# One change to a fused scan and two-layer feed-forward kernel: weight conversion handed out by need, an earlier fetch of constants, and whole units for the second tile

## The chip, the cores and the metric

The kernel runs on one core of a Trainium2 chip. The metric is the device time of one execution in microseconds (us), lower is better; for the kernel before it is the median of three runs.

## What is computed

```python
log_a = np.log(np.clip(a, 1e-06, 1.0))
for c in range(nc):                      # chunks of 32 along the sequence of 768
    ...
    L = np.exp(cum[:, :, :, None] - cum[:, :, None, :]) * causal
    y_intra = np.einsum('bhij,bhjd->bhid', CB * L, xc)
    y_inter = np.einsum('bhin,bhnd->bhid', Cc, state) * decay_to_i
    state = decay_full * state + np.sum(Bx, axis=2)
x = y.transpose(0, 2, 1, 3).reshape(B * S, H * D)          # 3072 tokens x 256
h = np.maximum(np.maximum(x @ w1, x @ w2), x @ w3)         # 256 -> 768
x = h @ w_out                                              # 768 -> 256
h = x @ v_in                                               # 256 -> 2048
g = np.maximum(h, 0.0) + alpha * np.minimum(h, 0.0)
out = g @ v_out                                            # 2048 -> 256
```

The scan has 4 batches, 8 heads, head width 32 and state 16. The weights arrive in 64-bit floats.

## The kernel before

The tokens are cut into six tiles of 512. A tile goes through layer 1 (`up1`, L586: three products with 256-wide weights, their maximum) and layer 2 (`up2`, L600: one product and the leaky maximum), each followed by a product back to 256 columns (`down`, L613). A *unit* is one 128-wide slice f of a layer's hidden width over one tile: 6 in layer 1, 16 in layer 2. Every product is done in two halves of each operand (`parts`, L567, whose matmul is L572): high by high, low weight by high, high weight by low, so 18 matmuls for `up1` (three weights, two row halves), 6 for `up2`, 6 for `down` (two halves of the output columns). After `up` the unit's result g is split into gh on ScalarE (ACT, L123) and gl on GpSimd (POOL, L124), and `down` of a unit follows two units later (`LAG`).

The phases run in the order of `PHASES` (L32): layer 1 of tiles 0 and 1, then layer 2 of tile t and layer 1 of tile t + 2 in turn. Tiles 0 and 1 of layer 1 are cut into units of 256 tokens (`SPLIT`, in the order `ORDER`), all others into 512 (`WHOLE`).

Two other kinds of work are put between the units.

**Weight conversion** (`convert`, L158). The weights come in 28 pieces of 512 KB: 12 of layer 1, 16 of layer 2. One piece takes four steps: a shift on VectorE (DVE, L163), a merge of the two words (DVE, L165), then the fetch of the piece three ahead into the staging tile just freed (L149, on the queue of SyncE, SP) and the high half on ACT (L169), then the low half on DVE (L171) and, for the next piece, a rebias on ACT (L156). Three staging tiles `st` go round. Sixteen steps are taken ahead of the first unit; from there `pace` = 1 asks for one step at each of four places of a layer 1 unit (after each of its three products and after `down`) and two of a layer 2 unit.

**Attention** (the scan), in 24 blocks of 128 tokens, four to a tile. The list `todo` holds its steps; a block has six: loads (b and c, 64 KB each, x 128 KB, and the decay rows e, 256 KB), transposes `att_t` (matmul L331), the exponentials `att_e` (ACT L400, then a causal select on POOL, L403), the state update `att_u` (matmul L455, DVE L461 and L467), the products `att_b` (matmul L422, multiplied into e on DVE, L427), and the output `att_y` (matmuls L496 and L504, whose halves go to xt on ACT L513 and DVE L514). `quota` (L558) says how many steps follow a unit, so that each unit's blocks are done `LEAD` = 6144 matmul columns ahead of it; a unit of layer 1 needs all blocks up to its last token. From block 12 on a wider form is used, for which `wide_sums` (L277) makes prefix sums with two triangular constants of 128 KB; it fetches them itself (L280) just ahead of the matmuls that read them (L285).

Only the start (`with tc.manual_schedule()`, L665 to L718) keeps the order in which it is written. Behind it a scheduling layer orders each engine's instructions, so that a step may stand well ahead of the place at which the code asks for it. Engines run their own list in order.

Of the kernel before, what the change touches and what calls it, by code (L numbers as in the profile page):

```python
# [19 lines left out]
P = 128  # L20
# [7 lines left out]
NF1, NF2 = FF1 // P, FF2 // P  # L28
NT = BT * S // 512

SPLIT, WHOLE = ((0, 256), (256, 256)), ((0, 512),)
PHASES = [(1, 0, SPLIT, 1), (1, 1, SPLIT, 1)]  # L32
for _t in range(NT):
    PHASES += [(2, _t, WHOLE, 1)] + [(1, _t + 2, WHOLE, 1)] * (_t + 2 < NT)

LEAD = 6144
START = 4
LAG = 2
NX = 3

C_ID, C_PAR, C_PM, C_N = 0, 128, 130, 132
C_TU, C_TS, C_TW, C_SEL, C_T = 0, 128, 256, 512, 1024
# [29 lines left out]
def fused(ctx: ExitStack, tc: tile.TileContext, x, a, B, C, w1, w2, w3, w_out, v_in, v_out, alpha, cst, out):  # L72
    nc = tc.nc
# [103 lines left out]
    steps = convert()  # L177
    ready = [0]

    def need(i):  # L180
        while ready[0] <= i:
            next(steps)

    def next_weights(n):
        for _ in range(n):
            next(steps, None)


    cum_d = dr.tile([NQ, BT * H, Q], F32, name="cum_d", bufs=1)
# [57 lines left out]
    def sums(half):  # L247

        ks = slice(3 * half, 3 * half + 3)
        qs = slice(6 * half, 6 * half + 6)  # L250
        cols = slice(3 * P * half, 3 * P * (half + 1))
        pc = ptile(ps_at, "at", (BT * H, 3 * P))
        for k in range(3):
            nc.tensor.matmul(pc[:, k * P:(k + 1) * P], s_la[:, 3 * half + k, :], tri_u, start=True, stop=True)
        yield
        nc.vector.tensor_copy(s_tot[:, qs].unsqueeze(2), pc.rearrange("p (k i) -> p k i", i=Q)[:, :, Q - 1:Q])
        nc.vector.tensor_copy(s_cum[:, cols], pc)
        nc.sync.dma_start(cum_d[qs].rearrange("k h i -> h k i"), s_cum[:, cols].rearrange("h (k i) -> h k i", i=Q))
        yield
        pf = ptile(ps_at, "at", (P, BT, 6))  # L260
        for b in range(BT):
            nc.tensor.matmul(pf[:, b, :], s_c[:BT * H, C_SEL + b * P:C_SEL + (b + 1) * P], s_tot[:, qs], start=True, stop=True)
        nc.scalar.activation(dec_f[:, :, qs], pf, AF.Exp)
        yield
        pt = ptile(ps_at, "at", (P, 3, BT * H))
        for k in range(3):
            nc.tensor.transpose(pt[:, k, :], s_cum[:, (3 * half + k) * P:(3 * half + k + 1) * P], ident[:BT * H, :BT * H])
        nc.scalar.activation(dec_c[:, ks].rearrange("p k b h -> p k (b h)"), pt, AF.Exp)
        nc.scalar.activation(ncum[:, ks].rearrange("p k b h -> p k (b h)"), pt, AF.Copy, scale=-1.0)
        yield  # L270
# [5 lines left out]

    def wide_sums(half):  # L277

        if half == 0:
            nc.sync.dma_start(s_c[:, C_TW:C_SEL], cst[:, C_N + C_TW:C_N + C_SEL])  # L280
        ks = slice(3 * half, 3 * half + 3)
        cols = slice(3 * P * half, 3 * P * (half + 1))
        pc = ptile(ps_at, "at", (BT * H, 3 * P))
        for k in range(3):
            nc.tensor.matmul(pc[:, k * P:(k + 1) * P], s_la[:, 3 * half + k, :], s_c[:, C_TW:C_TW + P], start=True, stop=True)  # L285
        nc.scalar.activation(s_a[:, cols], pc, AF.Copy)
        nc.sync.dma_start(cum_w[:, cols], s_a[:, cols])
# [229 lines left out]
    def rounds(r0):  # L517

        for r in range(r0, NR):
            def first(r=r):  # L520
                if r + 1 < NR:
                    att_l(r + 1)
                if r + 2 < NR:
                    att_a(r + 2)
            yield first, 0
            yield lambda r=r: att_y(r), r + 1
            if r + 1 < NR:
                yield lambda r=r: att_e(r + 1), 0
# [20 lines left out]
    def units_of(ph):  # L549

        layer, t, tokens = ph[:3]
        if len(tokens) == 1:
            cut = [(f, 0, 512) for f in range(NF1 if layer == 1 else NF2)]
        else:
            cut = [(f, *tokens[h]) for q, h in ORDER for f in (2 * q, 2 * q + 1)]
        return [(f, o, n, (24 if layer == 1 else 12) * n, (4 * t + (o + n) // P) * (layer == 1)) for f, o, n in cut]

    def quota(i):  # L558

        most, ahead, own = 0.0, 0, plan[i][3]  # L560
        for _, _, _, cols, blocks in plan[i:]:
            most = max(most, left(blocks) * own / max(own, ahead - LEAD))
            ahead += cols
        return most


    def parts(acc, wh, wl, rhs, first, last):  # L567
# [16 lines left out]
        return gh[:, :n], gl[:, :n]  # L584

    def up1(ph, f, o, n):  # L586
        t, pace = ph[1], ph[3]
        fs = slice(f * P, (f + 1) * P)
        g = un.tile([P, 512], F32, tag="g", name="g")[:, :n]
        for j in range(3):  # L590
            need(4 * (f // 2) + j)
            p = up_mm([w[:, j, :, fs] for w in w123], xt[t], o, n)
            if j == 0:
                nc.scalar.activation(g, p, AF.Copy)  # L594
            else:
                nc.vector.tensor_tensor(g, p, g, ALU.max)  # L596
            next_weights(pace)
        return halves(g, n)

    def up2(ph, f, o, n):  # L600
        t, pace = ph[1], ph[3]
        fs = slice(f * P, (f + 1) * P)
        g = un.tile([P, 512], F32, tag="g", name="g")[:, :n]
        need(4 * (NF1 // 2) + 2 * (f // 2))
        p = up_mm([w[:, :, fs] for w in vi], yt[t], o, n)
        nc.vector.tensor_scalar(g, p, 0.0, alph[:, f:f + 1], ALU.min, ALU.mult)  # L606
        nc.vector.scalar_tensor_tensor(g, p, 0.0, g, ALU.max, ALU.add)  # L607
        next_weights(pace)
        return halves(g, n, nc.vector if t == NT - 1 and f == NF2 - 1 else nc.gpsimd)

    acc = {}
# [108 lines left out]
    if True:  # L720
        nc.sync.dma_start(alph, alpha.rearrange("(k p) -> p k", p=P))
        todo += [(go, 0) for go in (
            lambda: att_a(2), lambda: (att_t(2), load(3)), lambda: att_e(2),
            lambda: att_u(2), lambda: att_b(2), lambda: att_a(3), lambda: (att_t(3), load(4)),
        )]
        todo.insert(SUMS, (lambda: list(sums(1)), 0))
        todo += rounds(2)
        for i, go in enumerate((lambda: wide_sums(0), lambda: wide_sums(1), wide_back)):
            todo.insert(WIDE + 3 * i, (go, 0))
        plan = [u for ph in PHASES for u in units_of(ph)]  # L730

        owed, at = 0.0, 0
        for ph in PHASES:
            layer, t, _, pace = ph
            up, end = (up1, end1) if layer == 1 else (up2, end2)
            pend = []
            for f, o, n, _, blocks in units_of(ph):
                until(blocks)
                pend.append((f, o, n, up(ph, f, o, n)))
                if carry:  # L740
                    carry.pop(0)()
                elif tail:
                    tail.pop(0)()
                if len(pend) > LAG:
                    down(ph, *pend.pop(0))
                next_weights(pace)
                owed += quota(at)
                at += 1
                while owed > 0.999 and todo:
                    owed -= 1  # L750
                    attend()
            for i, u in enumerate(pend):
                def go(ph=ph, u=u, finish=end if i == LAG - 1 else None):
                    down(ph, *u)
                    if finish:
                        finish(ph)
                carry.append(go)
        for go in tail:
            go()
        tail.clear()  # L760
        for u in pend[:-1]:
            down(ph, *u)
        f, _, _, g = pend[-1]
        for o, n in SPLIT:
            down(ph, f, o, n, [x[:, o:o + n] for x in g])
            end2(ph, o, n)
            while tail:
                tail.pop(0)()
# [25 lines left out]
```

## Time and profile before

| | |
|---|---|
| median of 3 runs | 569.25 us (569.04 to 570.7) |
| the profiled execution | 569.79 us, of which the profile's span is 568.0 us |
| PE (TensorE matmul) busy | 553.3 us, 97% of the span |
| DVE / ACT / POOL busy | 338.4 / 234.7 / 226.9 us |
| granted TensorE clock | full in all 40 slices of the span |
| chain that ended last | PE 85%, DMA 8%, DVE 3% |

In a profile's row for a group of instructions, `x18` is a count, `[0.83 <-DVE e L427]` says that the engine stood idle for 0.83 us and what ended that, and a name such as `up<-xt,w` gives the tile written and the tiles read. A busy PE is not always PE at its best: a matmul's row lasts until its last result is out, while the next one has begun.

### The profile page before, as it was taken

The page shows a single profiled execution, that of the slowest core. Times are in us where ns is not written, and L with a number is a line of the kernel's source. Part 1 is how long each engine was busy: PE and PEld are TensorE (multiplying, and loading weights), DVE is VectorE, ACT ScalarE, POOL GpSimd, SP SyncE. Part 2 cuts the span into 40 slices and gives each one's busy share as a digit, 9 for nine tenths or more (in the row PEclk, how much of TensorE's full clock was granted, in tenths as well). Part 3 has the DMA queues.
Part 4 walks back from the last instruction along what each step waited for, and adds up shares of the span by engine and source line. Part 5 has one row for each costly group of instructions (what it writes and reads, how often), then busy time and mean ns, then how long its engine had stood idle before and what let it go on. Part 6 is the DMA issues. An engine that isn't in the chain of part 4 may idle for free.

```text
span 568.0 us, 10190 instructions
## 1 busy us (share of the span) xinstructions
PE 553.3 (97%) x3754; PEld 446.3 (79%) x3754; DVE 338.4 (60%) x633; ACT 234.7 (41%) x598; POOL 226.9 (40%) x238
## 2 busy tenths in 40 slices
PE   8989999999999999999999999999999999999996
PEld 4769798897777887777787887787777888888885
DVE  5887899847564446765546664545664325555553
ACT  5667679744233334242543333534322222223222
POOL 2144343445444235453324553423444123444441
PEclk9999999999999999999999999999999999999999
DMA  7888887612213426325354325244110010000001
GB/s 145 222 164 161 233 214 211 144 30 38 31 43 87 111 66 140 86 59 136 73 134 111 89 50 139 65 113 112 38 55 1 1 37 2 0 2 18 20 0 37
DMA packets 118928, 48.53 MB, mean 85 GB/s; under 512 B 80736, under 2 KB 108832, under 8 KB 118880
## 3 DMA queue, kind: packets, MB, share of 16 engines
q1 hardware_dynamic: 118880, 47.90, 34.8%
q8 instruction: 29, 0.48, 0.4%
q14 instruction: 19, 0.16, 0.1%
HBM read 39.82 MB, written 8.06 MB: 84 GB/s over the span
## 4 chain that ended last, share of the span: by engine, by line
PE 85%; DMA 8%; DVE 3%; ACT 2%; issue 1%; POOL 1%; SPq 0%; DVEq 0%; ACTq 0%; POOLq 0%
PE up L572 45%; PE acc L572 30%; DMA st<-in_moe_w_out_dram 4%; DMA b<-in_B_dram 2%; DMA st<-in_moe_w_in_dram 1%; PE at L412 1%; PE at L483 1%; PE up L648 1%; PE at L331 1%; PE at L504 1%; PE at L422 1%; DVE v L165 1%; DMA e<-cum_w 1%; PE at L496 1%; PE at L480 1%
## 5 line engine op out<-in xcount | busy, mean ns | idle before, releaser
L124 POOL TENSOR_TENSOR gl<-g,gh 128x512 fp32r<-128x512 f32 (+1 forms) x143 | 173.0, 1210 | 262.8 <-ACT gh L123 236.2
L123 ACT ACTIVATE gh<-g 128x512 fp32r<-128x512 f32 (+1 forms) x144 | 85.6, 594 | 239.1 <-DVE g L607 157.9
L572 PE MATMUL up<-xt,w 128*128 128x256 f32 (+1 forms) x864 | 166.0, 342 | 3.3 <-ACT g L594 2.7
L572 PEld LDWEIGHTS up<-xt,w 128*128 128x128 f32 x864 | 134.5, 189 | 25.4 <-ACT g L594 3.5
L572 PE MATMUL up<-yt,vi 128*128 128x512 f32 x576 | 151.1, 396 | 0.0
L572 PEld LDWEIGHTS up<-yt,vi 128*128 128x128 f32 x576 | 105.4, 188 | 24.0 <-issue 2.0
L606 DVE TENSOR_SCALAR g<-up,alph 128x512 f32<-128x512 f32 x96 | 72.0, 750 | 87.4 <-PE up L572 81.5
L572 PE MATMUL acc<-gh,vo 128*128 128x512 f32 (+1 forms) x388 | 119.6, 389 | 0.6 <-DVE yt L634 0.5
L596 DVE TENSOR_TENSOR g<-up,g 128x256 f32<-128x256 f32 (+1 forms) x96 | 53.2, 554 | 69.2 <-PE up L572 67.9
L572 PEld LDWEIGHTS acc<-gh,vo 128*128 128x128 f32 x388 | 72.2, 188 | 16.3 <-DVE yt L634 1.4
L572 PE MATMUL acc<-gl,vo 128*128 128x512 f32 (+1 forms) x194 | 75.2, 388 | 0.0
L607 DVE SCALAR_TENSOR_TENSOR g<-up,g 128x512 f32<-128x512 f32 x96 | 66.3, 691 | 3.0
L572 PE MATMUL acc<-gh,wo 128*128 128x256 f32 (+1 forms) x192 | 49.2, 342 | 0.4 <-ACT gh L123 0.2
L572 PEld LDWEIGHTS acc<-gl,vo 128*128 128x128 f32 x194 | 36.4, 188 | 7.8 <-DVE gl L124 0.2
L572 PEld LDWEIGHTS acc<-gh,wo 128*128 128x128 f32 x192 | 32.5, 190 | 4.4 <-ACT gh L123 0.4
L594 ACT ACTIVATE g<-up 128x256 f32<-128x256 f32 (+1 forms) x48 | 23.4, 487 | 30.3 <-PE up L572 27.3
L572 PE MATMUL acc<-gl,wo 128*128 128x256 f32 (+1 forms) x96 | 32.5, 338 | 0.0
L395 ACT ACTIVATE e<-e,ncum 128x128 f32<-128x128 f32 x96 | 30.4, 391 | 3.5 <-DMA e<-cum_w 3.5
L514 DVE TENSOR_TENSOR xt<-at,xt 128x128 fp32r<-128x128 f32 x48 | 11.9, 286 | 20.2 <-ACT xt L513 20.2
L165 DVE SCALAR_TENSOR_TENSOR v<-st,v 128x512 uint32<-128x512 uint32 x28 | 21.6, 773 | 1.0 <-ACT st L156 0.5
L396 POOL TENSOR_SCALAR_AFFINE_SELECT e<-e 128x512 f32<-128x512 f32 x24 | 15.7, 653 | 16.2 <-ACT e L395 12.9
L400 ACT ACTIVATE e<-e,ncum 128x64 f32<-128x64 f32 x80 | 21.4, 342 | 1.1 <-DMA e<-cum_d 1.0
(120 smaller groups left out, 440.3 us busy)
## 6 DMA issues: line engine op xcount, KB each, us to landing
e<-cum_w SPq DMA_DIRECT2D x24, 256.0 KB, 4.1
st<-sc SPq DMA_DIRECT2D x48, 128.0 KB, 2.6
st<-in_moe_w_out_dram SPq DMA_DIRECT2D x11, 512.0 KB, 4.5
st<-in_moe_w_dram SPq DMA_DIRECT2D x9, 512.0 KB, 5.0
sc<-ts SPq DMA_DIRECT2D x12, 384.0 KB, 2.3
st<-in_moe_w_in_dram SPq DMA_DIRECT2D x8, 512.0 KB, 4.4
v<-sc SPq DMA_DIRECT2D x48, 64.0 KB, 2.4
out_dram<-st SPq DMA_DIRECT2D x12, 256.0 KB, 2.2
```

Of the source, the lines that this page charges most:

```text
L123: nc.scalar.activation(dst_h, src, AF.Copy)
L124: engine.tensor_tensor(dst_l, src, dst_h, ALU.subtract)
L165: nc.vector.scalar_tensor_tensor(v, hi, 3, v, ALU.logical_shift_left, ALU.bitwise_or)
L395: nc.scalar.activation(e[:, q, :], e[:, q, :], AF.Exp, bias=ncum[:, k, b, 4 * g + q:4 * g + q + 1])
L396: nc.gpsimd.affine_select(out=e, in_=e, pattern=[[0, 4], [1, P]], compare_op=ALU.is_ge, fill=0.0, base=0, channel_multiplier=-1)
L400: nc.scalar.activation(e[:, h, :], e[:, h, :], AF.Exp, bias=ncum[:, k, b, h:h + 1])
L514: nc.vector.tensor_tensor(xt[t][1][:, g, o], yp[g], xt[t][0][:, g, o], ALU.subtract)
L572: nc.tensor.matmul(acc, w, r, start=(first and i == 0), stop=(last and i == len(todo_) - 1), skip_group_check=True)
L594: nc.scalar.activation(g, p, AF.Copy)
L596: nc.vector.tensor_tensor(g, p, g, ALU.max)
L606: nc.vector.tensor_scalar(g, p, 0.0, alph[:, f:f + 1], ALU.min, ALU.mult)
L607: nc.vector.scalar_tensor_tensor(g, p, 0.0, g, ALU.max, ALU.add)
```

## The change

1. Tile 1 of layer 1 is cut into 6 units of 512 tokens in place of 12 of 256.
2. Past tile 0 the conversion steps are handed out by `quota_w`: at each place (`slot`) a fraction of a step is added to `owing`, sized so that each unit's pieces are converted `LEADW` = 12288 columns ahead of it. A unit has four places: in layer 1 one after each product and one behind `down`, in layer 2 two and two. Worked out from the formula, a place takes 0.96 to 0.98 of a step in tile 1 of layer 1 and 0.47 to 0.50 in layer 2 of tile 0, up to its unit 11, where the last step falls. Tile 0 of layer 1 keeps one step at each place.
3. The fetch of the wide constants moves from `wide_sums` into the eighth attention step (the one with block 3's transposes and block 4's loads).

```diff
-PHASES = [(1, 0, SPLIT, 1), (1, 1, SPLIT, 1)]
+PHASES = [(1, 0, SPLIT, 1), (1, 1, WHOLE, 0)]
 for _t in range(NT):
-    PHASES += [(2, _t, WHOLE, 1)] + [(1, _t + 2, WHOLE, 1)] * (_t + 2 < NT)
+    PHASES += [(2, _t, WHOLE, 0)] + [(1, _t + 2, WHOLE, 0)] * (_t + 2 < NT)
...
+LEADW = 12288
...
+    owing = [0.0, 0.0]
+
+    def slot():
+
+        owing[0] += owing[1]
+        while owing[0] > 0.999:
+            owing[0] -= 1
+            next_weights(1)
...
-        if half == 0:
-            nc.sync.dma_start(s_c[:, C_TW:C_SEL], cst[:, C_N + C_TW:C_N + C_SEL])
...
+    def quota_w(i):
+
+        most, ahead, own = 0.0, 0, plan[i][3]
+        for _, _, _, cols, _, pieces in plan[i:]:
+            most = max(most, (4 * pieces - done[0]) * own / max(own, ahead - LEADW))
+            ahead += cols
+        return most / 4
...
-            next_weights(pace)
+            slot()
...
+        todo[7] = (lambda go=todo[7][0]: (go(), nc.sync.dma_start(s_c[:, C_TW:C_SEL], cst[:, C_N + C_TW:C_N + C_SEL])), 0)
...
             for f, o, n, _, blocks, _ in units_of(ph):
                 until(blocks)
+                owing[1] = pace or quota_w(at)
```

Since the first unit of tile 1 now holds all 512 tokens, it needs blocks 4 to 7 where it needed 4 and 5. By `quota`'s formula the attention steps behind a unit of tile 0, from its fourth unit on, rise from about 2.2 to between 3.0 and 3.5 (the last unit's fall to 0.9), and the output of blocks 6 and 7 and what lies between moves from tile 1 into tile 0.

What the scheduling layer makes of it stands in three places. On DVE, the end of the conversion: before, with L163, L165 and L171 the conversion, L596 the maximum of layer 1 and L606 and L607 those of layer 2 (names: v and st staging, vi and vo weights of layer 2, g a unit's result):

```order
L165 SCALAR_TENSOR_TENSOR v<-st,v 128x512
L596 TENSOR_TENSOR g<-up,g 128x256
L171 TENSOR_TENSOR vo_116<-v,vo_115 128x512
L596 TENSOR_TENSOR g<-up,g 128x256 x2
L514 TENSOR_TENSOR xt_1959<-at,xt_1958 128x128 x2
L596 TENSOR_TENSOR g<-up,g 128x256 x4
L461 TENSOR_TENSOR u<-at,ct 128x128
L467 SCALAR_TENSOR_TENSOR u<-u,dec_f 128x64 x2
L596 TENSOR_TENSOR g<-up,g 128x256 x2
L427 TENSOR_TENSOR e<-at,e 128x256 x2
L606 TENSOR_SCALAR g<-up,alph 128x512
L607 SCALAR_TENSOR_TENSOR g<-up,g 128x512
```

and now (L167 and L173 are the conversion, L617 the maximum of layer 1, L627 and L628 those of layer 2):

```order
L617 TENSOR_TENSOR g<-up,g 128x512
L167 SCALAR_TENSOR_TENSOR v<-st,v 128x512
L439 TENSOR_TENSOR e<-at,e 128x256 x2
L173 TENSOR_TENSOR vo_116<-v,vo_115 128x512
L617 TENSOR_TENSOR g<-up,g 128x512 x2
L362 TENSOR_TENSOR bs<-at,ct 128x256
L627 TENSOR_SCALAR g<-up,alph 128x512
L628 SCALAR_TENSOR_TENSOR g<-up,g 128x512
```

In both, the last piece is converted ahead of layer 2's first maximum, though the code now asks for 23 of the 112 steps behind that phase's start. Eight maxima of tile 1, those of four units of 256 tokens, stood behind the last conversion; now two, those of the last unit of 512. Ahead of tile 1's first maximum stand the low halves of 18 pieces in both.

On SP, the fetch of the wide constants (`yt<-in_shape_constants`; xm is x, e<-cum_d the decay rows, L149 and L151 fetch weights). Before, it is the 56th issue, behind the loads of block 6:

```order
L217 DMA xm_105<-in_x_dram 64x8x32 [waits DMAHW5_49,PE_49]
L217 DMA xm_105<-in_x_dram 64x8x32 [waits DMAHW6_49,PE_49]
L280 DMA yt_120<-in_shape_constants_dram 128x256 [waits DMAHW7_49]
L149 DMA st<-in_moe_w_in_dram 128x2x256 [waits DMAHW0_49,DVE_49]
L149 DMA st<-in_moe_w_out_dram 128x2x256 [waits DMAHW1_49,DVE_49,Activation_49]
L287 DMA cum_w<-xt_119 32x384 [waits DMAHW2_49,Activation_49]
```

and now the 41st, behind those of block 4:

```order
L231 DMA xm_106<-in_x_dram 64x8x32 [waits DMAHW6_49]
L231 DMA xm_106<-in_x_dram 64x8x32 [waits DMAHW7_49]
L749 DMA yt_120<-in_shape_constants_dram 128x256 [waits DMAHW0_49]
L151 DMA st<-in_moe_w_dram 128x2x256 [waits DMAHW1_49,DVE_49,Activation_49]
L325 DMA e<-cum_d 64x512 [waits DMAHW2_49]
```

It has moved ahead of three fetches of weights, two blocks' e and two blocks' b, c and x.

On PE, the seam of the tenth and eleventh of tile 0's twelve units (L593 was L572 before, L467 L455, L434 L422, L508 L496, L516 L504), where block 6's state and products stood before:

```order
L593 MATMUL acc<-gl,wo_111 128x256
L508 MATMUL at<-cpt,u 64x64 x4
L516 MATMUL at<-e,xm_105 32x64 x16
L467 MATMUL at<-xm_106,bp 32x128 x4
L593 MATMUL up<-xt_305,w_0_109 128x256
L434 MATMUL at<-cs,bs 64x128 x8
L593 MATMUL up<-xt_305,w_0_109 128x256
L593 MATMUL up<-xt_305,w_1_110 128x256 x2
L593 MATMUL up<-xt_306,w_0_109 128x256 x2
```

Here block 6's output and block 7's state and products follow one another; block 7's output stands one unit later. Before, both outputs stood in tile 1.

## Rows read from the trace of the kernel before

**Rows 1.** Windows: stretch, length, busy us (count) of PE, PEld, DVE, ACT, POOL; clock; DMA share; GB/s

```profile
35.87:78.64 42.77, 40.08 (x485) 34.95 (x483) 33.93 (x78) 31.03 (x97) 17.65 (x26) 1.00 0.83 195
78.64:113.50 34.86, 32.49 (x357) 29.46 (x356) 31.91 (x70) 27.90 (x80) 15.97 (x21) 1.00 0.73 188
113.50:125.09 11.59, 11.59 (x151) 10.66 (x150) 4.68 (x14) 6.11 (x22) 6.58 (x11) 1.00 0.16 35
...
175.65:212.55 36.90, 36.90 (x199) 29.74 (x198) 17.06 (x31) 13.94 (x33) 11.22 (x12) 1.00 0.33 84
```

**Rows 2.** Chain of waits, 113 to 126 us: start, us, what

```profile
114.21 0.40 PE at L496 x16
114.61 0.58 PE at L504 x32
115.20 2.34 PE up L572 x18
117.54 0.72 PE acc L572 x6
118.26 2.16 PE up L572 x18
...
121.14 0.36 PE at L455 x8
...
124.56 0.60 PE at L422 x16
```

**Rows 3.** Chain of waits, 175 to 190 us (layer 1 of tile 2)

```profile
175.82 4.08 PE up L572 x18
...
181.50 4.31 PE up L572 x18
...
185.82 1.36 PE acc L572 x6
...
187.65 0.33 PE at L331 x3
```

**Rows 4.** Timeline of PE, around 95 and 110 us: start, us, what [idle before]

```profile
95.47 1.77 PE L572 MATMUL up<-xt,w 128*128 128x256 f32 x12 [0.80 <-ACT g L594]
...
110.59 2.67 PE L572 MATMUL up<-xt,w 128*128 128x256 f32 x16 [1.37 <-ACT g L594]
```

**Rows 5.** Chain of waits, 85 to 130 us

```profile
102.13 5.95 DMA st<-in_moe_w_out_dram
```

**Rows 6.** Timeline of PE, 57 to 59 us

```profile
58.13 0.81 PE L285 MATMUL at<-yt,la 128*32 128x128 f32 x6 [0.88 <-DMA yt<-in_shape_constants_dram]
```

**Rows 7.** Timeline of SP, 44 to 62 us

```profile
54.90 0.61 SPq L280 DMA_DIRECT2D yt<-in_shape_constants_dram  x1
```

**Rows 8.** Line L165, 20 to 125 us: count, ns min/median/max, first and last start

```profile
L165 DVE SCALAR_TENSOR_TENSOR v<-st,v x25: 673/683/1236, 22.4 to 111.5; 128x512 uint32<-128x512 uint32 x25
```

**Rows 9.** Windows of L165 alone: stretch, length, busy us (count)

```profile
20.50:35.87 15.37, 3.72 (x5) 1.00 0.86 157
35.87:56.63 20.76, 3.43 (x4) 1.00 0.86 168
56.63:78.64 22.01, 4.28 (x6) 1.00 0.81 221
78.64:113.50 34.86, 8.12 (x11) 1.00 0.73 188
```

**Rows 10.** Timeline of POOL and DVE, 64 to 66 us

```profile
64.72 0.82 POOL L124 TENSOR_TENSOR gl<-g,gh 128x256 fp32r<-128x256 f32 x1 [4.91 <-DMA e<-cum_d]
64.86 1.22 DVE L171 TENSOR_TENSOR vo<-v,vo 128x512 fp32r<-128x512 f32 x1
```

**Rows 11.** Timeline of ACT, DVE and PE, 37 to 42 us

```profile
37.33 2.00 ACT L400 ACTIVATE e<-e,ncum 128x64 f32<-128x64 f32 x8
...
41.33 0.76 DVE L427 TENSOR_TENSOR e<-at,e 128x256 f32<-128x256 f32 x2 [0.75 <-POOL e L403]
...
41.91 0.45 PE L496 MATMUL at<-cpt,u 32*64 32x64 f32 x8 [0.83 <-DVE e L427]
```

More of the change, by code (lines that the diff above doesn't have):

```diff
@@ L178, in fused @@
     ready = [0]
+    done = [0]
     def need(i):
         while ready[0] <= i:
-            next(steps)
+            next_weights(1)
     def next_weights(n):
         for _ in range(n):
+            done[0] += 1
             next(steps, None)
+    owing = [0.0, 0.0]
[3 more added lines that the diff above has]
+            owing[0] -= 1
+            next_weights(1)
     cum_d = dr.tile([NQ, BT * H, Q], F32, name="cum_d", bufs=1)
@@ L555, in units_of @@
             cut = [(f, *tokens[h]) for q, h in ORDER for f in (2 * q, 2 * q + 1)]
-        return [(f, o, n, (24 if layer == 1 else 12) * n, (4 * t + (o + n) // P) * (layer == 1)) for f, o, n in cut]
+        return [(f, o, n, (24 if layer == 1 else 12) * n, (4 * t + (o + n) // P) * (layer == 1),
+                 4 * (f // 2) + 4 if layer == 1 else 4 * (NF1 // 2) + 2 * (f // 2) + 2) for f, o, n in cut]
     def quota(i):
         most, ahead, own = 0.0, 0, plan[i][3]
-        for _, _, _, cols, blocks in plan[i:]:
+        for _, _, _, cols, blocks, _ in plan[i:]:
             most = max(most, left(blocks) * own / max(own, ahead - LEAD))
@@ L586, in up1 @@
     def up1(ph, f, o, n):
-        t, pace = ph[1], ph[3]
+        t = ph[1]
         fs = slice(f * P, (f + 1) * P)
@@ L596, in up1 @@
                 nc.vector.tensor_tensor(g, p, g, ALU.max)
-            next_weights(pace)
+            slot()
         return halves(g, n)
     def up2(ph, f, o, n):
-        t, pace = ph[1], ph[3]
+        t = ph[1]
         fs = slice(f * P, (f + 1) * P)
@@ L607, in up2 @@
         nc.vector.scalar_tensor_tensor(g, p, 0.0, g, ALU.max, ALU.add)
-        next_weights(pace)
+        slot()
+        slot()
         return halves(g, n, nc.vector if t == NT - 1 and f == NF2 - 1 else nc.gpsimd)
@@ L736, in fused @@
             pend = []
-            for f, o, n, _, blocks in units_of(ph):
+            for f, o, n, _, blocks, _ in units_of(ph):
                 until(blocks)
+                owing[1] = pace or quota_w(at)
                 pend.append((f, o, n, up(ph, f, o, n)))
@@ L745, in fused @@
                     down(ph, *pend.pop(0))
-                next_weights(pace)
+                slot()
+                if layer == 2:
+                    slot()
                 owed += quota(at)
```

## The prediction

> **What bounds the kernel now.** I read the windows by stage first. They are cut where the first matmul of a phase starts: tile 0 of layer 1 at 20.5 us, tile 1 at 78.64, layer 2 at 125.09, tile 2 of layer 1 at 175.65. From 113.5 us on PE is busy all the time, in layer 1 of tile 2 for 36.90 of 36.90 us [rows 1]. Behind that point only fewer or shorter matmuls help, and the change keeps them. Ahead of it PE stands idle for 42.77 - 40.08 = 2.69 us in tile 0 (from its fourth unit) and for 34.86 - 32.49 = 2.37 us in tile 1 [rows 1], with DVE busy for 31.91 of those 34.86 us. So tiles 0 and 1 of layer 1 are the place, and little more than 5 us of idle PE lies there.
>
> The second view is the chain, for what a unit costs. One of 256 tokens takes 2.16 us for its 18 up matmuls, or 2.34 where attention has come between, and 0.72 for its 6 down [rows 2]. One of 512 takes 4.08 or 4.31, and 1.36 [rows 3]. The third is the timeline of PE at its longest waits: 0.80 and 1.37 us in tile 1, both ended by ACT's copy of a product [rows 4], with a weight piece's landing of 5.95 us in the chain ahead of the second [rows 5], and 0.88 us in tile 0 on the wide constants [rows 6]. The fourth is the merge of the conversion, L165: 25 of them from 22.4 to 111.5 us [rows 8], so 89.1 / 24 = 3.71 us a piece, but unevenly: 15.37 / 5 = 3.1, then 20.76 / 4 = 5.2, 22.01 / 6 = 3.7 and 34.86 / 11 = 3.2 [rows 9].
>
> **The change, part by part.** *Whole units in tile 1.* Like against like, 12 x (2.16 + 0.72) = 34.6 against 6 x (4.08 + 1.36) = 32.6 us, or 12 x (2.34 + 0.72) = 36.7 against 6 x (4.31 + 1.36) = 34.0. That is -2.0 or -2.7; I take **-2.4**, since both kinds occur. PE bounds tile 1's second half wholly [rows 1], so this lies on the path. A 256-column matmul costs 2.16 / 18 = 120 ns in the row and a 512-column one 227. The Trainium skill (TensorE: Matmul & The Clock Gate, section Back-to-back issue gap) gives 262 and 518 cycles for them, at 2.4 GHz 109 and 216 ns, so that width would be worth only 288 x 0.109 - 144 x 0.216 = 0.3 us, as an estimate of that page. The rows hold both widths, and they decide.
>
> *The wide constants.* The fetch was issued at 54.90 us [rows 7] and PE waited 0.88 us for it [rows 6]. It now stands 15 issues earlier on SP, two blocks' loads ahead, so it lands before it is asked for: **-0.9**, or 0 at the other end. What it is moved past (three fetches of weights, two blocks' loads) is put back once by one issue, 0.61 us [rows 7], which the ring of three staging tiles and the two units between an e load and its use hide; without that cover, +0.6.
>
> *Attention moved into tile 0.* Outputs 6 and 7 at 0.40 + 0.58 each, one state update 0.36, one set of products 0.60 [rows 2] and one of transposes 0.33 [rows 3], together 3.25 us of PE, go from tile 1 to tile 0; block 10's transposes and block 13's output also come forward by a phase. PE's sum is the same: 0. The moved steps bring their loads, 512 KB a block, on a DMA share of 0.83 [rows 1]. What is new is tightness: blocks 4 and 7 now have their output one unit behind their exponentials. The row for that is block 3, done so today: exponentials from 37.33 us, DVE's multiply held for POOL until 41.33, and PE idle for 0.83 until 41.91 [rows 11]. A unit here takes PE 2.88 to 3.06 us and the other steps, less than those 4.6. Two such waits are 1.7; I take **+1.2**, ends 0 and +3.
>
> *Conversion steps by need.* The code would put 23 steps into layer 2 of tile 0, but by DVE's list the last piece is still converted ahead of layer 2's first maximum. So DVE, ACT and the fetches keep the work of all 28 pieces ahead of that phase, and 10 of them fall on tile 1 as before. Its waits of 2.37 us [rows 1] came where PE, ACT and the fetch met. The tile asks for a piece every 3.7 us (10 in some 37 us: 33.3 of units and 3.6 of attention, which is two state updates, products and transposes and one output), where the ring gave one every 3.2 [rows 9]; that speaks for their going. Against it, DVE was busy for 31.91 + 4.68 = 36.6 us in tile 1 [rows 1] and has as much PE time to fit into. I take half of the waits, **-1.2**, ends -2.4 and 0.
>
> Sum: -2.4 - 0.9 + 1.2 - 1.2 = **-3.3 us**, so a span of 564.7 and an execution of 566.5 where the profiled one was 569.79 (span 568.0). That execution stands 0.54 above the median of the three, 569.25; I forecast a median of 569.25 - 3.3 = **566.0 us**. Its own ends are about 564 and 568.
>
> **The rivals.** *No new wait (chance 0.18).* Tile 0 hides what it takes over and tile 1 runs as layer 1 of tile 2 does: -2.7 - 0.9 - 2.4 = -6.0, 563.2 us. For it: that tile has the same units and PE never idle [rows 1]. Against it: no conversion stands beside them there.
>
> *DVE held by POOL (0.17).* A conversion's subtraction that starts 0.14 us behind POOL's gl takes 1.22 us, 0.54 more than the 0.68 usual on such an operation, and ends that much behind gl [rows 8, 10]. The Trainium skill (SBUF — State Buffer, section Who interferes with whom) says that a DVE instruction with two SBUF inputs and a GpSimd one that reads SBUF exclude each other for the whole instruction; the row agrees. Tile 1 now has six gl of 512 tokens. If each holds DVE once by 0.54, 3.2 us come onto an engine without room, and the gain shrinks to -0.1: 569.2 us. Against it: there were twelve of 256, so there are half as many to meet.
>
> *The staging ring falls behind, slower (0.09).* The merges set a floor to layer 2's start, since now only one unit of maxima stands behind the last: about 1.1 us behind it. At today's 3.71 us a piece that is 112.5 us, far ahead of the 121.8 that the forecast needs. The floor shows at (121.8 - 1.1 - 22.4) / 24 = 4.1 us a piece and makes the kernel slower from (125.09 - 1.1 - 22.4) / 24 = 4.23. A stretch of 5.2 exists [rows 9], where loads of attention and weights share SP's queue, and tile 0 now has half as much attention again to its end. If 12 pieces go at 5.2 from 35.87 us and 8 at 3.7: 35.87 + 62.4 + 29.6 + 1.1 = 129.0, +3.9, 573.1 us. Against it: 22.01 / 6 = 3.7 right behind that stretch, with attention as dense.
>
> **How the numbers follow.** The forecast has 0.56. Some 0.3%, 1.7 us, is what a measurement here can tell from no change. Faster by more: the forecast but for 0.04 of it, and the first rival, 0.70. Within: that 0.04 and the second rival, 0.21. Slower: the third, 0.09. The range holds the first rival and the second and leaves out the third and a little at either end: 562.8 to 569.4.
>
> **What would show it.** Right: in the profile after, layer 2's first matmul stands near 122 us; tile 1 lasts 37 to 39 us where it lasted 46.45, and tile 0 from its fourth unit 46 to 47 where it lasted 42.77; L285's successor waits for no DMA; the 512-column forms of L572 gain 144 matmuls; behind 175 us nothing is shorter. Wrong: tile 0 beyond 49 us (the moved attention waits more than block 3 did), merges at 4.2 us a piece or more, or DVE's conversion rows in tile 1 above 1 us in the mean with PE idle for DVE or ACT.

## The result, and the profile after

The changed kernel takes 561.81 us (median of four runs, 561.73 to 562.16) where the kernel before took 569.14 in the same session: the ratio is 0.9866, 95% interval 0.9848 to 0.9884, so 7.6 us less (6.6 to 8.7); by the two medians it is 7.3. The forecast was 566.0 with a range from 562.8 to 569.4. The gain is more than twice the forecast's 3.3, and the first rival ("no new wait", 563.2) came nearest. The profiled execution took 561.73 us (span 560.0).

The page of the kernel after, busy time and the chain that ended last:

```profile
PE 548.5 (98%) x3609; PEld 437.6 (78%) x3610; DVE 338.0 (60%) x621; ACT 233.2 (42%) x586; POOL 224.2 (40%) x232
...
PE 91%; ACT 3%; DVE 2%; SPq 1%; DMA 1%; issue 1%; POOL 0%; DVEq 0%; POOLq 0%; ACTq 0%
```

PE is busy for 4.8 us less, so the other 3.2 of the span's 8.0 us are idle time of PE that is gone. DMA's share of the chain falls from 8% to 1%. The windows after, cut as in [rows 1] where a phase's first matmul starts (tile 0 of layer 1 from its fourth unit, tile 1, layer 2 of tile 0, layer 1 of tile 2, layer 2 of tile 1; same columns):

```profile
35.49:81.44 45.95, 43.66 (x599) 37.64 (x598) 36.20 (x89) 34.12 (x113) 19.34 (x31) 1.00 0.82 184
81.44:117.76 36.32, 36.32 (x248) 28.41 (x247) 34.32 (x61) 28.81 (x73) 18.12 (x19) 1.00 0.70 188
117.76:168.61 50.85, 50.85 (x392) 39.67 (x391) 32.81 (x57) 16.87 (x41) 23.44 (x22) 1.00 0.22 46
168.61:206.77 38.16, 38.16 (x223) 30.24 (x222) 18.48 (x34) 14.79 (x38) 12.28 (x14) 1.00 0.39 98
206.77:255.85 49.08, 48.95 (x274) 38.67 (x271) 32.07 (x58) 18.04 (x47) 23.59 (x23) 1.00 0.40 101
```

And of the kernel before, tile 1 as a whole and the phases that [rows 1] does not hold:

```profile
78.64:125.09 46.45, 44.08 (x506) 40.12 (x504) 36.60 (x82) 34.01 (x101) 22.55 (x31) 1.00 0.59 150
125.09:175.65 50.56, 50.56 (x396) 39.41 (x393) 32.80 (x57) 16.21 (x40) 22.68 (x22) 1.00 0.22 45
212.55:263.29 50.74, 50.60 (x297) 39.13 (x296) 32.78 (x61) 18.77 (x51) 25.04 (x24) 1.00 0.43 100
```

Tile 1 goes from 46.45 to 36.32 us, -10.13, and PE is never idle in it (36.32 of 36.32). Tile 0 from its fourth unit goes from 42.77 to 45.95, +3.18; its idle time falls from 2.69 to 45.95 - 43.66 = 2.29. The three units ahead of that take 0.4 less. So layer 2 starts at 117.76 where it started at 125.09: 7.33 of the span's 8.0 us are won by there. Behind it little moves: +0.29, +1.26 and -1.66 for the next three phases.

The chain of waits after, in tile 1, gives the unit's cost, as [rows 2] and [rows 3] did:

```profile
81.60 4.11 PE up L593 x18
...
97.00 1.36 PE acc L593 x6
...
105.41 4.42 PE up L593 x18
109.82 1.36 PE acc L593 x6
111.18 0.60 PE at L434 x16
111.78 4.54 PE up L593 x18
116.32 1.36 PE acc L593 x6
```

Nothing but PE stands in that chain. The waits of PE over the whole span after (us in total, times, longest), down to the first that ACT's copy of a product ends:

```profile
PE up L685 <- DVE g L690: 1.3, 1, 1.3
PE at L434 <- DVE xt L526: 0.9, 1, 0.9
PE up L396 <- DVE g L394: 0.9, 1, 0.9
PE at L508 <- DVE e L439: 0.8, 1, 0.8
PE up L593 <- ACT xt L525: 0.6, 1, 0.6
PE up L593 <- ACT g L615: 0.5, 1, 0.5
```

The two waits of tile 1 on ACT's copy [rows 4] and the one on the wide constants [rows 6] are gone, block 3's 0.83 [rows 11] stays. (The 1.3 in the first line and the 0.9 in the third stand ahead of 20 us.) One is new: 0.9 in tile 0, near 73 us, in front of a set of attention's products (L434), on the low half of an output (L526). The merges of the conversion (L167) stand as in [rows 8], at (114.4 - 22.4) / 24 = 3.83 us a piece:

```profile
L167 DVE SCALAR_TENSOR_TENSOR v<-st,v x25: 674/682/1414, 22.4 to 114.4; 128x512 uint32<-128x512 uint32 x25
```

### The profile page after: what moved, and what is told of

Its sections match the earlier page's. It is cut to its first block, busy times and chain, and to the rows that moved or that the text cites. A ratio compares the mean times of both kernels' runs of the same rounds, so it can differ in the third digit from the quotient of the medians.

```text
span 560.0 us, 9853 instructions
## 1 busy us (share of the span) xinstructions
PE 548.5 (98%) x3609; PEld 437.6 (78%) x3610; DVE 338.0 (60%) x621; ACT 233.2 (42%) x586; POOL 224.2 (40%) x232
## 4 chain that ended last, share of the span: by engine, by line
PE 91%; ACT 3%; DVE 2%; SPq 1%; DMA 1%; issue 1%; POOL 0%; DVEq 0%; POOLq 0%; ACTq 0%
PE up L593 49%; PE acc L593 32%; PE at L495 1%; PE at L424 1%; PE at L343 1%; PE up L670 1%; DMA b<-in_B_dram 1%; PE at L434 1%; PE at L516 1%; ACT e L412 1%; PE at L492 1%; DVE v L167 1%; PE up L685 1%; SPq L231 1%; PE at L508 1%
## 5 line engine op out<-in xcount | busy, mean ns | idle before, releaser
L593 PE MATMUL up<-xt,w 128*128 128x512 f32 (+1 forms) x756 | 162.2, 365 | 1.1 <-ACT xt L525 0.6
L593 PE MATMUL up<-yt,vi 128*128 128x512 f32 x576 | 150.8, 396 | 0.0
L593 PEld LDWEIGHTS up<-xt,w 128*128 128x128 f32 x756 | 126.9, 189 | 26.1 <-issue 2.6
L627 DVE TENSOR_SCALAR g<-up,alph 128x512 f32<-128x512 f32 x96 | 72.0, 750 | 87.5 <-PE up L593 82.3
L593 PEld LDWEIGHTS up<-yt,vi 128*128 128x128 f32 x576 | 105.6, 188 | 23.9 <-issue 2.2
L593 PE MATMUL acc<-gh,vo 128*128 128x512 f32 (+1 forms) x388 | 119.2, 388 | 0.0
L617 DVE TENSOR_TENSOR g<-up,g 128x512 f32<-128x512 f32 (+1 forms) x84 | 51.4, 612 | 62.9 <-PE up L593 61.8
L593 PEld LDWEIGHTS acc<-gh,vo 128*128 128x128 f32 x388 | 72.4, 188 | 15.3 <-DVE yt L656 0.4
L593 PE MATMUL acc<-gl,vo 128*128 128x512 f32 (+1 forms) x194 | 75.2, 388 | 0.0
L628 DVE SCALAR_TENSOR_TENSOR g<-up,g 128x512 f32<-128x512 f32 x96 | 66.3, 691 | 3.1
L593 PE MATMUL acc<-gh,wo 128*128 128x512 f32 (+1 forms) x168 | 47.5, 367 | 0.2 <-ACT gh L125 0.2
L593 PEld LDWEIGHTS acc<-gl,vo 128*128 128x128 f32 x194 | 36.4, 188 | 7.8 <-DVE gl L126 0.2
L615 ACT ACTIVATE g<-up 128x512 f32<-128x512 f32 (+1 forms) x42 | 22.5, 535 | 28.2 <-PE up L593 24.3
L593 PEld LDWEIGHTS acc<-gh,wo 128*128 128x128 f32 x168 | 29.6, 189 | 5.2 <-ACT gh L125 0.4
L593 PE MATMUL acc<-gl,wo 128*128 128x512 f32 (+1 forms) x84 | 30.5, 364 | 0.0
L526 DVE TENSOR_TENSOR xt<-at,xt 128x128 fp32r<-128x128 f32 x48 | 12.2, 287 | 19.8 <-ACT xt L525 19.6
L167 DVE SCALAR_TENSOR_TENSOR v<-st,v 128x512 uint32<-128x512 uint32 x28 | 21.6, 771 | 0.7
L158 ACT ACTIVATE st<-st 128x512 f32<-128x512 f32 x28 | 18.9, 677 | 3.6 <-DMA st<-in_moe_w_out_dram 2.1
```

What stands on the lines that cost most here:

```text
L158: nc.scalar.activation(hi, hi, AF.Prelu, scale=2.0 ** -112, alpha=2.0 ** 32)
L167: nc.vector.scalar_tensor_tensor(v, hi, 3, v, ALU.logical_shift_left, ALU.bitwise_or)
L526: nc.vector.tensor_tensor(xt[t][1][:, g, o], yp[g], xt[t][0][:, g, o], ALU.subtract)
L593: nc.tensor.matmul(acc, w, r, start=(first and i == 0), stop=(last and i == len(todo_) - 1), skip_group_check=True)
```

## The experiments

Sixteen kernels ran in four sessions, each compared with the kernel before on the same chip; gains in us are the ratio less 1, times 568.5. In many executions of these sessions, of the kernel before as well, the mean granted clock is below 1.0 (0.994 to 1.0 in that kernel's runs; the last section shows where it falls). So most intervals are 1 to 1.5 us to either side, and the changed kernel itself stands at 0.9895 (0.9873 to 0.9917), which is -6.0 us, -4.7 to -7.2. The expectations put tile 1's waits before at 3.0 us (1.1 to 4.3 in five profiles); length less busy time, by which the text goes, gives 2.37 (0.89 to 3.48).

**The three parts, each alone, and the attention's move alone.** Edits of the kernel before: e1 takes the first hunk's WHOLE for tile 1 and keeps its `pace` of 1; e2 takes `slot` and `quota_w` past tile 0 and keeps tile 1 SPLIT; e3 takes the two hunks on the fetch; e4 changes the blocks that a unit asks for. The lines of e1 and e4:

```diff
-PHASES = [(1, 0, SPLIT, 1), (1, 1, SPLIT, 1)]
+PHASES = [(1, 0, SPLIT, 1), (1, 1, WHOLE, 1)]
```
```diff
-(4 * t + (o + n) // P) * (layer == 1)
+(4 * t + (4 if t == 1 else (o + n) // P)) * (layer == 1)
```

Whole units alone:

> The kernel before with tile 1 of layer 1 in units of 512 tokens, and nothing else of the change: the conversion keeps one step at each place, the wide constants are fetched where they were. Three theories on the 7.3 us. WIDTH (wider units take fewer columns' worth of time, 3.1 us, and leave the other engines so much room that tile 1's 3.0 us of waits go with them): -5.5 to -6.5 us, tile 1 with PE idle for under 0.3 us. NEED (the waits went because the conversion is handed out by need): -2.5 to -3.5 us, with 2 to 3 us of idle PE left in tile 1. ATTENTION (the waits went because two blocks' outputs left tile 1 for tile 0): as WIDTH here, since whole units bring that move with them; the run that moves the attention alone parts the two.

Measured: 564.37 us, ratio 0.9922 (0.9896 to 0.9948), -4.4 us, between what WIDTH and what NEED expected. Conversion by need alone:

> The kernel before with the conversion steps handed out by need past the first tile, and nothing else: tile 1 stays in units of 256 tokens, the constants are fetched where they were. PE's order is that of the kernel before, row for row; only steps on DVE, ACT, POOL and SP change places. NEED: -2 to -3.5 us, tile 1 from 46.45 to some 43.5 us. WIDTH and ATTENTION: within 0.5 us of the kernel before, tile 1 with its 2.4 us of idle PE as before.

Measured: 567.4 us, 0.9982 (0.9962 to 1.0003), -1.0, again between the two. The constants alone:

> The kernel before with the fetch of the wide constants moved to the eighth attention step, and nothing else. All three theories: the wait of 0.88 us on the constants goes, -0.5 to -1.0 us. If the transfer was hidden behind something that then shows (the next piece of weights or block 7's loads), -0.3 to 0.

Measured: 568.69 us, 1.001 (0.9987 to 1.0032): no gain where all theories expected one. The attention alone:

> The kernel before with one entry of the plan changed: every unit of tile 1 asks for blocks 4 to 7, also the first ones that read only 4 and 5, so that the two blocks' outputs move from tile 1 into tile 0 as in the change, while the units stay 256 tokens wide and the conversion and the constants stay as they were. ATTENTION: the waits of tile 1 go, -1.5 to -3 us, tile 1 some 3 us of attention and 2 to 3 us of waits shorter (some 41 us), tile 0 some 3 to 4 us longer. WIDTH: tile 1 keeps most of its waits or tile 0 takes them over; within 1 us of the kernel before. The forecast's own term for this move was +1.2 us.

Measured: 569.28 us, 1.0015 (0.9987 to 1.0043), +0.9, which does not contradict the forecast's term of +1.2 and cannot be told from nothing either. The windows of tile 1 in the four, in this order:

```profile
82.98:121.27 38.29, 36.32 (x248) 28.48 (x247) 35.61 (x63) 29.40 (x73) 19.33 (x21) 1.00 0.70 183
```
```profile
78.12:121.88 43.76, 42.87 (x506) 39.81 (x504) 36.08 (x82) 34.01 (x101) 23.94 (x31) 1.00 0.62 158
```
```profile
77.81:125.41 47.60, 44.12 (x503) 40.27 (x503) 37.98 (x84) 35.16 (x106) 22.50 (x32) 1.00 0.57 148
```
```profile
84.36:128.38 44.02, 41.64 (x392) 38.08 (x391) 36.95 (x76) 31.58 (x88) 19.46 (x26) 1.00 0.63 160
```

ATTENTION falls: with the outputs gone from tile 1, PE still idles there for 44.02 - 41.64 = 2.38 us. With whole units alone 1.97 are left, in one wait. The timelines of PE and of ACT there (start, us, what, idle before):

```profile
108.91 1.42 PE L595 MATMUL up<-xt,w 128*128 128x512 f32 x5 [1.97 <-ACT g L617]
```
```profile
107.19 0.68 ACT L158 ACTIVATE st<-st 128x512 f32<-128x512 f32 x1 [1.93 <-DMA st<-in_moe_w_in_dram]
107.76 0.62 ACT L171 ACTIVATE vo<-v 128x512 fp32r<-128x512 f32 x1
108.28 0.58 ACT L617 ACTIVATE g<-up 128x512 f32<-128x512 f32 x1
```

ACT's list runs in order. The rebias (L158) of a weight piece that had not landed held it for 1.93 us, and behind it stood the copy that frees a product's buffer for PE. The kernel before has the same picture ahead of its wait of 1.37 us at 110.59 [rows 4], in front of the copy at 110.15:

```profile
108.10 0.67 ACT L156 ACTIVATE st<-st 128x512 f32<-128x512 f32 x1 [1.56 <-DMA st<-in_moe_w_out_dram]
```

So I thought that the handing out by need might have moved that rebias, and took each part back from the change.

**The change, and each part taken back.** Edits of the changed kernel: f1 none; f2 `pace` 1 in layer 1 and 0.5 in layer 2 in place of 0; f3 the fetch back in `wide_sums`; f4 SPLIT for tile 1.

> The changed kernel once more, beside the three runs that take one part of it back. All theories: -6.5 to -8 us against the kernel before. If the granted clock dips behind block 3's output here too (42 to 50 us, as in the profiles of the four single parts), -5 to -7 us, with tile 1 still free of waits.

> The changed kernel with the conversion again at one step in each place (half a step in layer 2's doubled places), whole units and the constants' fetch kept. PE's order is the changed kernel's, row for row; on DVE, ACT, POOL and SP 33 rows differ, all in tile 1. TOGETHER (the width makes room, but a late weight piece still stops ACT in front of a copy that PE needs, as in the run with whole units alone, where PE stood for 1.97 us; the handing out by need moves that piece's rebias behind the copy): tile 1 with one wait of 1 to 2.5 us, so 1 to 2.5 us slower than the change. WIDTH: tile 1 without a wait over 0.3 us, within 0.5 us of the change.

> The changed kernel with the fetch of the wide constants back in wide_sums; whole units and handing out by need kept. If the earlier fetch is worth its 0.9 us: 0.5 to 1 us slower than the change, with PE waiting for the constants in tile 0. If the wait only comes or not by how the transfers fall (it is absent in the run with whole units alone, whose fetch stands at the old place): within 0.4 us.

> The changed kernel with tile 1 again in units of 256 tokens; the earlier fetch and the handing out by need kept. WIDTH: 5.5 to 6.5 us slower than the change, so 1 to 2 us faster than the kernel before, tile 1 with 2 us of idle PE or more. TOGETHER: 4 to 5 us slower than the change, tile 1 near the 43.75 us that it took with handing out by need alone, 1 us of waits left.

Measured: f1 562.81 us, 0.9895; f2 562.42 us, 0.9898 (0.988 to 0.9917); f3 563.84 us, 0.9929 (0.9902 to 0.9956); f4 568.06 us, 1.0002 (0.9979 to 1.0025). So f3 is 0.34%, 1.9 us, slower than f1, more than expected but with as much uncertainty, and f4 is 1.07%, 6.1 us, slower, as WIDTH had it. The windows of tile 1, f1 to f4:

```profile
80.75:116.89 36.14, 36.14 (x249) 28.41 (x247) 34.54 (x61) 28.72 (x73) 17.84 (x19) 1.00 0.69 186
```
```profile
81.29:117.94 36.65, 36.53 (x248) 28.38 (x247) 34.74 (x62) 29.04 (x73) 18.68 (x19) 1.00 0.70 187
```
```profile
83.18:120.49 37.31, 36.58 (x248) 28.36 (x247) 35.03 (x60) 29.08 (x71) 19.06 (x21) 1.00 0.70 185
```
```profile
77.68:124.29 46.61, 44.08 (x503) 40.28 (x503) 37.86 (x84) 35.26 (x106) 24.12 (x32) 1.00 0.59 151
```

TOGETHER falls with f2: without the handing out by need tile 1 has 36.65 - 36.53 = 0.12 us of idle PE and the time is the change's. The kernel before, e1, e2, e3, f2, f3, f4 and the change are the eight ways to have or not have each of the three parts, so each part has four pairs that differ in it alone. Whole units: -0.78, -1.12, -0.53 and -1.07%, in the mean -0.88%, **5.0 us**. The clock is no rival for that: the mean granted clock of a version's runs is 0.9962 to 0.9973 in all eight. By need: -0.18, -0.08, +0.07 and -0.03%, in the mean a gain of 0.3 us, less than can be told from nothing. The constants: +0.10 and +0.20% beside narrow units, -0.24 and -0.34% beside whole ones, each pair within its own uncertainty, so at most 1 to 2 us, and only there. In f3 PE waits for them more than before the change:

```profile
58.95 0.81 PE L299 MATMUL at<-yt,la 128*32 128x128 f32 x6 [1.68 <-DMA yt<-in_shape_constants_dram]
```

That wait was not there in every kernel with the fetch at its old place (e2's timeline, with narrow units, and e1's, with whole ones, have none; before has 0.88): it hangs on how the transfers of an execution fall.

Idle PE in tile 1 (length less busy) with narrow units was 2.37 before, 0.89, 3.48, 2.38 and 2.53 in e2, e3, e4 and f4; with whole ones 0 in the change and f1, 0.12, 0.73 and 1.97 in f2, f3 and e1. In the mean that is 2.33 against 0.56, a difference of 1.8; with the 3.2 us by which PE's busy time falls (next section) it makes the 5.0. Single profiles overlap: e2 with narrow units idles less than e1 with whole ones.

**More whole units.** If width pays, it should pay in tile 0. g1 cuts tile 0's last two slices whole, g2 its last four:

```diff
 g1:
-            cut = [(f, *tokens[h]) for q, h in ORDER for f in (2 * q, 2 * q + 1)]
+            cut = [(f, *tokens[h]) for q, h in ORDER[:4] for f in (2 * q, 2 * q + 1)] + [(f, 0, 512) for f in (4, 5)]
 g2:
+            cut = [(f, *tokens[h]) for h in (0, 1) for f in (0, 1)] + [(f, 0, 512) for f in (2, 3, 4, 5)]
```

> The changed kernel with the last third of tile 0 cut the same way: its last four units of 256 tokens (two slices, two halves) become two of 512. By the rows of a unit that is 4 x 2.88 = 11.5 against 2 x 5.44 = 10.9, so WIDTH gives 0.6 to 0.9 us on PE, and whatever waits stood in that stretch go too (0.9 us at 72 us in the changed kernel's profile): 0.6 to 1.8 us faster than the change. If the outputs of blocks 4 to 7 and the conversion come late there instead, 0 to 1 us slower.

> The changed kernel with tile 0 in four units of 256 tokens (the first two slices, both halves) and then four of 512. WIDTH alone gives twice the last one, 1.2 to 1.8 us. Against it the second half of the tile is asked for two units earlier, so the output of blocks 2 and 3 falls due some 5.8 us earlier, where PE already waits for block 3 (0.8 us near 41 us): 1 to 3 us slower than the change if that decides, 1 to 2 faster if the smaller need for weights (4 pieces in place of 8 by the fourth unit) decides.

Measured: g1 561.66 us, 0.9881 (0.9856 to 0.9906), not to be told from the change's 0.9895; g2 565.87 us, 0.9955 (0.9933 to 0.9976), 3.4 slower than the change. In g1 layer 2 starts at 117.07 where it starts at 116.89 in f1, so what the width gives is spent ahead of it; how stays open. In g2 the tile has four waits of 0.8 to 1.3 us between 28 and 41 us, and the granted clock is 0.50 from 36 to 46 us; the mean clock of its runs is 0.986 where the change's is 0.997. How much of the 3.4 us is the clock's and how much the waits' was not parted, so g2 does not price whole units in tile 0. No version ran that beats the change beyond the uncertainty.

**Why the waits go with width.** A product is six matmuls into one buffer, which is free again when ACT or DVE has read it. In a unit of 512 it gives PE 1.36 us of work where a narrow one gives 0.72. So with three buffers PE can run ahead of the readers by 2.72 us in place of 1.44 (RUN-AHEAD). The other reading is that these engines have less to do (RATE). The first try took a buffer from attention's three (before: g3, the change: g4):

```diff
-    ps_up = pool("ps_up", 3, space=PSUM)
+    ps_up = pool("ps_up", 4, space=PSUM)
...
-    ps_at = pool("ps_at", 3, space=PSUM)
+    ps_at = pool("ps_at", 2, space=PSUM)
```

> The kernel before with four buffers for the up products in place of three, and two for attention's in place of three. RUN-AHEAD (tile 1's waits are ACT's or DVE's copies that come later than the products PE can run ahead by: two of 0.72 us in units of 256 tokens, two of 1.36 in units of 512): with three of 0.72 ahead, tile 1's waits shrink from 3.0 (1.1 to 4.3 in the five profiles with narrow units) to 1.5 or less, though the units stay narrow, and the time falls by 1 to 2 us if attention does not miss its buffer. RATE (ACT and DVE have too much to do in tile 1 with twelve units of 256 tokens): tile 1's waits as before, time as before or worse.

> The changed kernel with the same exchange of buffers, which prices the buffer taken from attention where the up products have no wait in tile 1 to lose. Both theories: the change's time plus that price, 0 to 2 us slower than the change. RUN-AHEAD: the kernel before with four must come out better against its own base than this one by the 1 to 2 us of waits.

Measured: g3 577.22 us, 1.0153 (1.0126 to 1.018); g4 581.57 us, 1.0236 (1.0201 to 1.027). Both lose most of it ahead of tile 1, which starts at 86.36 and 102.04 us where it started at 78.64 and 81.44, with the clock lowered in stretches; that the buffer taken from attention is the reason is likely, not shown. Tile 1 of g3:

```profile
86.36:132.89 46.53, 45.09 (x542) 40.30 (x542) 36.17 (x84) 32.40 (x97) 19.91 (x29) 1.00 0.58 137
```

Its 46.53 - 45.09 = 1.44 us of idle PE is what RUN-AHEAD expected, but narrow units with three buffers had 0.89 to 3.48, so that decides nothing. The second try takes one product buffer away in tile 1 alone (h2 of the change, h4 of the kernel before; h1 and h3, their bases, have False in the last line):

```diff
+    def uptile(shape):
+        if ups[1]:
+            return ps_up.tile(shape, F32, tag="up", name="up", bufs=2)
+        ups[0] += 1
+        if ups[0] % 3:
+            return ps_up.tile(shape, F32, tag="up", name="up", bufs=2)
+        return ps_up.tile(shape, F32, tag="upx", name="upx", bufs=1)
...
+            ups[1] = ph[:2] == (1, 1)
```

> The changed kernel with its three up buffers named as two and one, used in the same turn, as the base of the next run. The scheduling layer orders some steps of tile 0 in another way for it, so the time may differ from the change by up to 2 us; tile 1 with waits under 0.5 us.

> The base just ahead of it, but tile 1 of layer 1 uses two of the three up buffers; every engine's order is the same. PE can then run ahead by one product of 1.36 us in place of two, about what two narrow products of 0.72 give. RUN-AHEAD: tile 1's waits come back, 1.5 to 4 us of idle PE, and the time rises by as much. RATE: under 0.7 us of idle PE in tile 1, time within 0.7 us of the base.

> The kernel before with its three up buffers named as two and one, used in the same turn, as the base of the next run. Within 2 us of the kernel before; tile 1 with 1 to 4.3 us of waits.

> The base just ahead of it, but tile 1 uses two of the three up buffers; every engine's order is the same. PE can run ahead by one product of 0.72 us in place of two. RUN-AHEAD: tile 1's waits grow by 3 us or more, time likewise. RATE: within 1 us of the base.

Measured: h1 563.55 us, 0.9911 (0.9893 to 0.9929); h2 566.49 us, 0.9953 (0.9938 to 0.9969); h3 570.12 us, 1.0027 (1.0014 to 1.0039); h4 572.89 us, 1.0067 (1.0049 to 1.0085). The windows of tile 1 of h1 and of h2:

```profile
81.83:118.44 36.61, 36.54 (x249) 28.42 (x247) 34.83 (x63) 29.98 (x76) 19.92 (x19) 1.00 0.68 183
```
```profile
83.12:123.82 40.70, 37.49 (x248) 28.17 (x247) 34.99 (x63) 30.55 (x77) 20.50 (x21) 1.00 0.64 171
```

DVE and ACT do the same instructions in the same order for the same time (34.8 and 35.0, 30.0 and 30.6 us), and PE's idle time goes from 0.07 to 3.21 us; the kernel is 0.42%, 2.4 us, slower, at the same mean clock (0.9958 and 0.9955). So for whole units RUN-AHEAD is shown: with the same work on ACT and DVE, the third buffer's 1.36 us hides their late reads. What made them late can be read in part in h2's timelines, of PE, ACT and DVE near 110 us, and of PE at its longest wait there:

```profile
110.32 0.96 PE L604 MATMUL up<-xt,w 128*128 128x512 f32 x3 [0.91 <-DVE g L628]
114.45 1.66 PE L604 MATMUL up<-xt,w 128*128 128x512 f32 x6 [1.13 <-ACT g L626]
```
```profile
109.22 0.68 ACT L169 ACTIVATE st<-st 128x512 f32<-128x512 f32 x1 [2.69 <-DMA st<-in_moe_w_out_dram]
```
```profile
109.24 0.43 DVE L176 TENSOR_SCALAR v<-st 128x512 uint32<-128x512 uint32 x1 [1.60 <-DMA st<-in_moe_w_out_dram]
109.58 0.68 DVE L628 TENSOR_TENSOR g<-up,g 128x512 f32<-128x512 f32 x1
```

At 110.32 it is again a late weight piece, behind whose shift the maximum stands. This piece was later than any in h1's tile 1 (2.69 against 0.99 us on ACT), so not all of the 3.21 us need be the buffer's doing; the 2.4 us between the runs' medians carry the verdict. The other four waits, 2.30 us in sum, end on ACT's copy. The longest, 1.13, comes while ACT works off its list without a break from 110.90 on (conversion, gh, attention's exponentials). In the change ACT waits for a piece for 0.98 us without PE noticing:

```profile
105.60 0.68 ACT L158 ACTIVATE st<-st 128x512 f32<-128x512 f32 x1 [0.98 <-DMA st<-in_moe_w_out_dram]
```

With narrow units, in e2, ACT waits for a piece for 0.86 us at 105.35 and then works without a break up to the copy at 107.43, for which PE stands idle for 0.89. How late the pieces are differs from profile to profile, though: ACT's longest wait for one in tile 1 is 0.98 and 0.20 us in the change's two profiles and 1.56 in the kernel before. So a part of tile 1's lost waits may be that in these profiles there was less lateness to bear.

For narrow units the pair h3 and h4 is less plain: h4 is 0.40% slower than h3, but its profile has 47.27 - 44.97 = 2.30 us of idle PE in tile 1 against 47.04 - 45.53 = 1.51, not the 3 more that were expected, and 1.5 us longer in tile 0, where the two programs are alike. The mean clock of h4's runs is a little lower besides (0.9940 against 0.9952). That narrow units wait for want of run-ahead is argued, not shown.

## Why the prediction was too small

- **Place and direction: right.** All but 0.7 of the span's 8.0 us is won ahead of layer 2, in tiles 0 and 1; tile 0 lasts 45.95 (46 to 47 forecast), and no DMA holds L285's successor. Tile 1 at 36.32 (37 to 39) and layer 2's start at 117.76 (122) are beyond the forecast. "Behind 175 us nothing is shorter" holds only in sum: layer 2 of tile 1 is 1.66 shorter where layer 1 of tile 2 is 1.26 longer.
- **"Whole units in tile 1", -2.4: right in kind, too small.** PE's busy time in tile 1 falls by 44.08 - 36.32 = 7.76. Of that, 3.25 is attention moved out, by the prediction's own count, and 2 x (1.36 - 0.72) = 1.28 is the `down` of the last two units, now wide, which runs in layer 2's phase either way. That leaves 3.2, where the ends were 2.0 and 2.7. The 0.3 that the prediction worked out from the Trainium skill (TensorE: Matmul & The Clock Gate, section Back-to-back issue gap), whose figures are those of an isolated matmul, is refuted as a price for this loop: 4.11 / 18 = 228 ns a matmul agrees with the 227 of [rows 3], and the narrow one's 120 ns stood in [rows 2].
- **"Conversion steps by need", -1.2: the step that failed.** Half of tile 1's 2.37 us of waits was put down to the order of the conversion. All of it went, and not for that reason: handing out by need, added alone or taken back, moves 0.3 us in the mean, while whole units move 5.0. I had set the cause of the longest wait right (a late piece in front of ACT's copy, [rows 4, 5]) but asked only whether the pieces would come sooner. They come no faster (3.83 us each, before 3.71). What changed is how long a lateness PE can bear, for which the sum had nothing, and that belongs to the width: h1 and h2 show it for whole units, for narrow ones it is argued. The 3.2 us a piece that the term used counts the merge that began at 78.25 us in both windows; ten in 34.86 us are 3.5, still below the 3.7 asked for.
- **Attention moved into tile 0, +1.2: too large in the change, by itself not contradicted** (e4: +0.9, -0.7 to +2.4). In the change the two waits like block 3's did not come at blocks 4 and 7; one of 0.9 came elsewhere, and tile 0's idle time fell by 0.4 in all with the constants' 0.9 in it, so some 0.5 was new.
- **The constants, -0.9: right in the profile, not as a price.** The wait is gone, but by itself the edit gains nothing (e3), and beside whole units 1 to 2 us at most.
- **The rivals.** "No new wait" had tile 1 without idle PE, which is what happened, with -2.7 and -2.4 for width and waits; the profile has -3.2 and -2.4. Its -6.0 us is what the second measurement of the change gave (-6.0, -4.7 to -7.2); the forecast's -3.3 lies outside both. "DVE held by POOL" did not decide: DVE's busy time in tile 1 fell from 36.60 to 34.32 us. The Trainium skill's rule (SBUF — State Buffer, section Who interferes with whom) is not refuted by that: a merge at 102.05 us that took 1414 ns against the usual 682 ended 0.55 us behind the gl that ran when it began and looks like such a hold, but PE waits for none in tile 1. "The staging ring falls behind" did not come, at 3.83 us a piece.
- **What the sum had no term for.** Width 3.2, tile 1's waits 2.4 and tile 0's idle time 0.4 make 6.0 of the profile's 8.0 us. Some 0.4 more is idle time elsewhere, and 4.8 - 3.2 = 1.6 us of PE's busy time went outside layer 1's products, in small pieces whose cause stays open.

## What to carry to other kernels

Widening a unit of work bought two things here: less PE time per column (227 ns for 512 where two of 256 took 240), and a longer run-ahead in a ring of the same number of buffers. Price the second by the longest lateness that the reader's in-order queue shows, against the time that the other buffers hold. Where a wait's cause is a late arrival, ask how much lateness the waiting engine can bear after the change, not only whether the arrival comes sooner.

## What the runs showed of the hardware

The granted clock of TensorE fell in tile 0 in some executions and not in others, behind the same waits of PE. The windows of h1 and then of h2 from 36 and 44 us, whose programs are alike up to there, and whose longest waits there are alike (1.34 and 0.73 us in h1, 1.28 and 0.74 in h2, both on POOL):

```profile
36.00:44.00 8.00, 5.93 (x70) 4.64 (x69) 5.97 (x13) 4.51 (x15) 4.30 (x6) 1.00 0.81 201
44.00:50.00 6.00, 6.00 (x95) 5.41 (x94) 3.49 (x10) 3.96 (x15) 1.33 (x3) 1.00 0.93 163
```
```profile
36.00:44.00 8.00, 5.97 (x76) 4.83 (x80) 5.29 (x13) 4.52 (x15) 4.32 (x6) 0.90 0.93 166
44.00:50.00 6.00, 6.00 (x68) 5.06 (x59) 3.20 (x9) 3.00 (x10) 0.84 (x2) 0.57 0.76 153
```

PE was idle for 2.07 and 2.03 us in the first window; in the one execution the clock stays at 1.00 (2.4 GHz), in the other it falls toward the end of that window (0.90) and is 0.57 in the next, between that level and the lower one of 1.2 GHz, so for most of the stretch at the lower. Of f1's six runs the two with a mean clock of 1.0 took 560.85 and 560.93 us, the one with 0.992 took 564.4. That is some 3 us which the comparisons of these kernels carry as scatter. In the profiles of e1 to e4 and f4 the fall begins between 42 and 44 us, behind the wait of 0.83 us at block 3's output; in h2 to h4 it begins there too, behind the waits on POOL (in h4 on a DMA as well). The change, f1 to f3 and g1 have the same 0.83 us, and the clock stays at 1.00. Why it falls in one execution and not in the next stays open.
